# Block-sparse attention with a Strassen-form MLP: batch 1's side steps re-placed, and half of the spread of batches 2 and 3 moved to ScalarE

## The chip, the cores and the metric

One core of a Trainium2 chip runs the kernel. The time is the device time of one execution in microseconds (us), taken as the median of several runs. Engines go by the profile's names: PE is TensorE (matmuls; PEld its weight loads), DVE is VectorE, ACT is ScalarE, POOL is GpSimd, SP is SyncE, which issues DMAs. Each engine works through its own instructions in the order of the program, and waits on semaphores for the others.

## The reference

Four batches, 8 heads, 768 positions, head size 64. Every position attends to the 31 positions around it and to 24 block summaries (maximum of the keys, mean of the values over blocks of 32); then an MLP with a swish gate follows.

```python
k_sum = k.reshape(B, H, nb, block, D).max(axis=3)      # block = 32, nb = 24
v_sum = v.reshape(B, H, nb, block, D).mean(axis=3)
scores_l = scale * q @ k.T, kept where |i - j| < 16
scores_s = scale * q @ k_sum.T + log(block)
a = softmax(concatenate([scores_l, scores_s]))
x = (a @ concatenate([v, v_sum])) -> (B * S, H * D)     # 3072 x 512
h = x @ w_in                                            # 512 x 2048
out = (h * sigmoid(beta * h)) @ w_out                   # 2048 x 512
```

Inputs and output are float32; the kernel multiplies in bf16.

## The kernel before, in words

The batches go one after another. The MLP of batch b fills TensorE, and the attention of batch b+1 is threaded between its output matmuls. Heads go in pairs: four groups g = 0 to 3. Positions go in 12 query tiles of 64, six to a half u = 0, 1.

**The order is written out by hand.** `main` is the list of TensorE's large steps, and `sides` a list of small steps with a place each, from the table `AT`. `run` emits main step i, then every side step whose place is below i + 1 (in the order of the places). A place of 28.05 thus means: behind main step 28. The main steps:

- 0 to 7 `h_two`: two h tiles of batch 0, first half of the positions; step p writes the two-bank tile big1, big2, big0 in turn (p = 7 writes big2, p = 6 big1)
- 8 to 23 `h_half`: 16 h tiles of batch 0, second half, one at a time in one1, big0, one0 in turn
- 24 to 39 `o_atom`: outputs of batch 0, four position tiles (0, 3, 4, 1) in four steps of 4 matmuls each, in one0 or one1; behind the fourth ScalarE copies the result out and SP stores it
- 40 to 46: the last two position tiles of batch 0 as seven products of a Strassen form (`products`, numbered 1, 6, 5, 4, 2, 7, 3)
- from 47 on, 37 steps for each of batches 1, 2 and 3: 16 `h_step` (h tiles of all 768 positions) and 21 products (three tiles t of seven; the first two of t = 0 are `first` and `then`). Batch 1 has 47 to 83, batch 2 84 to 120, batch 3 121 to 157.

Batch 1's attention therefore stands between main steps 8 and 40, batch 2's between 47 and 81, batch 3's between 84 and 117.

PSUM has the single banks one0 and one1, the double banks big1 and big2, and a pair that is big0 during the h tiles and two single banks acc0, acc1 during the products. Product 1 and product 2 share one0, products 6 and 7 one1, product 4 acc0, products 5 and 3 acc1. ScalarE empties products 1, 5 and 2 (`gather`, L683); VectorE the others.

**The side steps that the change touches** (`n` is the batch):

- `kt`, `qt` (`kt_pe` L387, `qt_pe` L396), batch 1 alone: two groups' keys or queries, loaded as whole rows (`krow`, `qrow`, by GpSimd's queue, in `more_loads`), are transposed by TensorE into a double bank, and copied out: keys by VectorE into `kw`, the 96-key windows of each query tile, with 8 copies in all; queries into `qn`, one copy per group by the engine given in `cps`
- `km` (`km_pe` L392): block maxima of one group (VectorE, L357) and their copies into `kw` (GpSimd, L365)
- `vc` (`v_cast`, L456, GpSimd): values to bf16 in `ve`; `vo` (`v_odd_dma`, L466): two DMAs on SP that write the same values 64 positions on into `vo`
- `sc` (`scores`, L429): 12 small matmuls per group and half, u = 0 into big2 and u = 1 into big1; then ScalarE's exponential (L447) into `e`
- `mk` (`mask_e`, L449): VectorE multiplies `e` by the window mask
- `vm` (`vm_all`, L482): block means of the values by TensorE, copied to `vm_sb` by VectorE and ScalarE in turn
- `sp` (`spread`, L492): copies the block means into rows 96 to 127 of `vo` and `ve` for two groups: per call 4 copies of 32 partitions by 768 elements
- `av` (`av_pair`, L865): the value products of one group, 24 matmuls, into big1 for even and big2 for odd groups, then VectorE's normalisation (`norm`, L530) into `xn`
- `xd` (`x_dma`, L550): `xn` transposed into `xT` by a DMA on ScalarE's queue (group 2 of batch 3 by TensorE); `xT` is what the next h tiles read
- `exp`, `silu`: loading of ScalarE's function table; `ws`, `hs`: VectorE's sums for the Strassen form
- `av0`, `x0`: value products and transposes of batch 0's second half; `clear` with `more_masks`: fills and mask

Of the kernel before, what the change touches and what calls it, by code (L numbers as in the profile page):

```python
# [13 lines left out]
    'loads': [2.306],  # L14
    'av0': [1.99, 3.661, 4.754],
    'x0': [5.759, 6.564],
    'scale': [8.171, 16.158, 16.833, 21.634],
    'clear': [6.428, 6.644],
    'kt': [10.122, 8.68],
    'km': [17.109, 13.223, 16.831, 23.85],  # L20
    'qt': [26.508, 26.967],
    'late': [32.254],
    'ws': [23.447, 26.164, 38.352, 39.431],
    'hs0': [36.284, 36.98, 42.604, 40.783],
    'vc1': [26.849, 25.757, 27.058, 30.017],
    'vo1': [27.153, 26.475, 30.624, 30.427],
    'exp1': [26.482],
    'sc1': [28.05, 28.06, 30.05, 30.06, 31.438, 31.448, 33.219, 33.904],
    'mk1': [28.082, 28.092, 30.899, 30.909, 32.558, 32.75, 33.826, 34.448],
    'silu1': [34.957],  # L30
    'vm1': [30.622],
    'sp1': [31.039, 33.384],
    'av1': [35.473, 35.88, 37.299, 37.483],
    'xd1': [36.323, 36.794, 40.874, 39.001],
    'hs1': [52.172, 56.695, 58.36, 62.056, 63.409],
# [13 lines left out]
    'sc2': [64.902, 64.912, 67.132, 67.349, 69.423, 69.507, 71.144, 71.507],  # L49
    'mk2': [64.907, 67.547, 69.019, 69.041, 70.656, 70.74, 74.611, 74.621],  # L50
    'silu2': [83.261],
    'vm2': [69.738],
    'sp2': [70.773, 71.834],
    'av2': [73.1, 73.251, 76.15, 76.759],
# [14 lines left out]
    'exp3': [100.49],  # L69
    'sc3': [100.954, 100.964, 104.012, 104.199, 106.253, 106.263, 107.654, 107.71],  # L70
    'mk3': [101.397, 102.413, 107.921, 107.97, 106.952, 108.221, 108.907, 110.666],
    'silu3': [112.501],
    'vm3': [107.308],
    'sp3': [107.454, 109.743],
    'av3': [110.088, 110.664, 114.187, 114.973],
# [27 lines left out]
def kernel(  # L103
# [10 lines left out]
    nc = tc.nc  # L114
    ctx.enter_context(tc.manual_schedule())
    P = 128
# [14 lines left out]
    J6 = S // P  # L131
# [162 lines left out]
    def more_masks():  # L294
        nc.vector.tensor_copy(out=mask[:], in_=band[:, None, :].to_broadcast([P, NT, QT]))
        nc.vector.memset(mask[0:W, 0], 0.0)
        nc.gpsimd.affine_select(out=mask[:, NT - 1], in_=mask[:, NT - 1], compare_op=ALU.is_ge, fill=0.0,
                                base=QT + W - 1, pattern=[[0, QT]], channel_multiplier=-1)
        nc.vector.memset(mask[NK:NK + nb], 1.0)

# [190 lines left out]

    def spread(gg):  # L492
        r = slice(NK, P)
        s = slice(2 * gg, 2 * gg + 2)
        for tt in (vo, ve):
            for h in range(2):
                nc.vector.tensor_copy(out=tt[r, s, h * J6:(h + 1) * J6, 0:D],
                                      in_=vm_sb[r, h, s, None, :].to_broadcast([P - NK, 2, J6, D]))

# [403 lines left out]
    at("loads", [more_loads])  # L903
    at("av0", [lambda: av_two(0, 1, one), lambda: av_two(2, 1, one[1:]), lambda: av_two(3, 1, one[:1])])
    at("x0", [lambda: x_two(0, 1, dve_cp, one[0]), lambda: x_two(2, 1, dve_cp, one[1])])
# [3 lines left out]
    at("km", [lambda g=g: km_pe(g, nc.gpsimd) for g in range(G)])  # L909
    at("qt", [lambda i=i: qt_pe(1, (2 * i, 2 * i + 1), 1 + i, (dve_cp, act_cp)) for i in range(2)])  # L910
    at("late", [late_tiles])
# [3 lines left out]
    for b in range(1, B):  # L915
# [18 lines left out]
        at("vm" + n, [lambda b=b: vm_all(scope["c"] if b > 1 else big[0], VMC)])  # L934
        at("sp" + n, [lambda i=i: spread(i) for i in range(2)])
        at("av" + n, [lambda g=g, b=b: av_pair(b, g, big[1 + g % 2]) for g in range(G)])
# [34 lines left out]
```

## Time and profile before

| | |
|---|---|
| median of 3 runs | 214.05 us (213.79 to 214.35) |
| profiled execution, its own time | 214.43 us |
| its span, first to last instruction | 211.7 us |
| granted TensorE clock | 0.997 |
| PE busy | 201.2 us (95%) |
| DVE busy | 140.7 us (66%) |
| ACT busy | 118.5 us (56%) |
| POOL busy | 62.3 us (29%) |
| moved by DMA | 33.92 MB, mean 160 GB/s |

Times in the views count from the first instruction. A row of a timeline has start, duration, engine, line of the kernel, operation, what it writes and reads (buffer numbers left out, so that big stands for big0, big1 and big2), partitions and elements, and how many were merged; in brackets the idle time of the engine before it and the instruction that ended it. A DMA that an engine issues is marked with q (ACTq, SPq). In groups by line the two numbers behind the bar are busy us and mean ns of one.

### The profile page before, as it was taken

How to read it: one execution, taken by the hardware profiler on the slowest of the kernel's cores; microseconds unless marked ns; L12 is line 12 of the kernel's file. 1: busy time of each engine (PE TensorE's matmuls, PEld its weight loads, DVE VectorE, ACT ScalarE, POOL GpSimd, SP SyncE). 2: the span in 40 equal slices, each digit the busy share in tenths (PEclk: the TensorE clock that was granted, in tenths of full speed). 3: DMA queues.
4: the chain of work that ended last, by engine and by line, in shares of the span. 5: the costliest groups of instructions: out<-in, count | busy, mean ns of one | idle time of the engine just before them, and what ended most of it. 6: DMA issues, size and time to landing. Idle time of an engine off the chain costs nothing.

```text
span 211.7 us, 5771 instructions
## 1 busy us (share of the span) xinstructions
PE 201.2 (95%) x2387; PEld 140.0 (66%) x2393; DVE 140.7 (66%) x324; ACT 118.5 (56%) x181; POOL 62.3 (29%) x94
## 2 busy tenths in 40 slices
PE   7889999999898999999999999999999999999993
PEld 2477656554545685566888865657788855668882
DVE  4587575899669980858999721998689704464132
ACT  2357876588588113966972138768763129662210
POOL 7708990001720017431520161553401100000111
PEclk9999999999999999999999999999999999999998
DMA  6999999999988988999689969999524920000242
GB/s 119 188 224 177 169 197 191 206 208 213 154 211 206 217 190 214 242 181 214 135 207 235 207 179 292 196 193 188 133 105 29 186 99 3 0 0 3 99 99 99
DMA packets 78393, 33.92 MB, mean 160 GB/s; under 512 B 60688, under 2 KB 75424, under 8 KB 78368
## 3 DMA queue, kind: packets, MB, share of 16 engines
q1 hardware_dynamic: 61968, 23.92, 54.5%
q0 software_dynamic: 7424, 7.34, 21.8%
q10 hardware_dynamic: 8976, 2.30, 7.9%
q8 instruction: 18, 0.29, 0.6%
q14 instruction: 7, 0.06, 0.1%
HBM read 27.37 MB, written 6.29 MB: 159 GB/s over the span
## 4 chain that ended last, share of the span: by engine, by line
PE 70%; DVE 14%; ACT 7%; issue 4%; DMA 3%; POOL 1%; POOLq 0%; DVEq 0%
PE big L601 28%; PE one L665 13%; PE acc L665 9%; PE big L579 5%; ACT e L447 4%; PE one L616 3%; DMA qrow<-in_q_dram 3%; DVE kw L371 2%; PE one L601 2%; DVE qn L371 2%; DVE w_out_sb L337 2%; DVE km L357 2%; DVE e L451 2%; PE big L512 1%; DVE t_sb L646 1%
## 5 line engine op out<-in xcount | busy, mean ns | idle before, releaser
L601 PE MATMUL big<-xT,w_in_sb 128*128 128x384 bf16 x360 | 60.5, 326 | 0.0
L601 PEld LDWEIGHTS <-w_in_sb 128*128 128x128 bf16 x384 | 37.5, 98 | 25.1 <-issue 0.7
L612 ACT ACTIVATE h_sb<-big,beta_sb 128x768 bf16<-128x768 f32 x45 | 39.6, 904 | 25.8 <-PE big L601 25.7
L665 PEld LDWEIGHTS <-h_sb 128*128 128x128 bf16 x320 | 30.7, 98 | 4.9 <-issue 0.5
L646 POOL TENSOR_TENSOR o_sb<-p,u 128x256 f32<-128x256 f32 x10 | 7.3, 728 | 88.7 <-DVE u L646 73.3
L665 PE MATMUL one<-w_out_sb,h_sb 128*128 128x256 bf16 x240 | 30.4, 273 | 0.2 <-ACT p L368 0.2
L447 ACT ACTIVATE e<-big,bias 128x768 bf16<-128x768 f32 x32 | 27.2, 899 | 5.4 <-PE big L426 3.4
L665 PEld LDWEIGHTS <-s_sb 128*128 128x128 bf16 x240 | 23.2, 98 | 2.8
L646 DVE TENSOR_TENSOR s_sb<-h_sb 128x768 bf16<-128x768 bf16 (+2 forms) x16 | 7.8, 488 | 23.4 <-ACT h_sb L612 23.4
L646 DVE TENSOR_TENSOR u<-one,p 128x256 f32<-128x256 f32 x20 | 8.4, 421 | 15.7 <-PE one L665 15.3
L456 POOL CAST ve<-vst 128x832 bf16<-128x832 f32 (+2 forms) x16 | 14.5, 924 | 14.2 <-DMA vst<-in_v_dram 10.8
L368 ACT COPY o_sb<-one 128x256 f32<-128x256 f32 (+1 forms) x14 | 6.1, 433 | 18.4 <-PE one L665 10.1
L451 DVE TENSOR_TENSOR e<-e,mask 128x768 bf16<-128x768 bf16 x24 | 13.4, 584 | 3.8 <-ACT e L447 3.7
L616 PE MATMUL one<-w_out_sb,h_sb 128*128 128x512 bf16 x59 | 14.2, 380 | 0.7 <-issue 0.6
L365 POOL COPY kw<-km 128x288 bf16<-128x288 bf16 x12 | 7.5, 627 | 24.8 <-DVE km L357 14.4
L361 DVE TENSOR_REDUCE km<-kT 128x24 bf16<-128x768 bf16 x12 | 11.3, 945 | 1.9 <-ACT kT L368 1.8
L539 DVE TENSOR_TENSOR xn<-big,r 128x768 bf16<-128x768 f32 x12 | 11.5, 957 | 0.4
L579 PE MATMUL big<-xT,w_in_sb 128*128 128x384 bf16 x64 | 11.6, 327 | 0.0
L665 PE MATMUL acc<-t_sb,h_sb 128*128 128x256 bf16 x80 | 10.9, 273 | 0.0
L646 DVE TENSOR_TENSOR s_sb<-h_sb,s_sb 128x768 bf16<-128x768 bf16 (+2 forms) x16 | 10.1, 630 | 0.5
L665 PE MATMUL one<-t_sb,s_sb 128*128 128x256 bf16 x80 | 10.4, 273 | 0.0
L665 PE MATMUL acc<-t_sb,s_sb 128*128 128x256 bf16 x80 | 10.4, 273 | 0.0
(145 smaller groups left out, 306.1 us busy)
## 6 DMA issues: line engine op xcount, KB each, us to landing
out_dram<-o_sb SPq DMA_DIRECT2D x19, 256.0 KB, 2.6
vst<-in_v_dram SPq DMA_DIRECT2D x13, 336.0 KB, 5.0
kst<-in_k_dram SPq DMA_DIRECT2D x8, 384.0 KB, 5.1
qst<-in_q_dram SPq DMA_DIRECT2D x8, 384.0 KB, 4.5
w_in_sb<-in_moe_w_in_dram POOLq DMA_DIRECT2D x4, 512.0 KB, 7.1
w_out_sb<-in_moe_w_out_dram POOLq DMA_DIRECT2D x4, 512.0 KB, 13.4
vo<-ve SPq DMA_DIRECT2D x12, 107.2 KB, 2.8
vst<-in_v_dram SPq DMA_DIRECT2D x3, 416.0 KB, 8.0
```

Of the source, the lines that this page charges most:

```text
L361: nc.vector.tensor_reduce(out=km[g][:, NK:NK + nb], in_=kT[g][:, W:W + S].rearrange("p (n f) -> p n f", f=block), op=ALU.max, axis=AX.X)
L371: nc.vector.tensor_copy(out=o, in_=i)
L447: nc.scalar.activation(out=e[:], in_=s[:, :, 0:HS], func=ACTF.Exp, bias=bias[:, 0:1], scale=scale)
L451: nc.vector.tensor_mul(out=e.rearrange("p h (m q) -> p h m q", q=QT), in0=e.rearrange("p h (m q) -> p h m q", q=QT), in1=(mask2 if b > 1 e ...
L456: eng.tensor_copy(out=ve[:, g, lo:hi, 0:D], in_=vst[g][:, lo:hi])
L539: nc.vector.tensor_mul(out=x[:, 3 * us[0]:3 * us[0] + 3 * n].rearrange("p (k j) h d -> p k (j h) d", k=n), in0=tv[:, :, :, 0:D], in1=r[:, ...
L579: nc.tensor.matmul(t[:, 0:HS], w_in_sb[:, ki, i * P:(i + 1) * P], xT[:, ki, 0:HS], start=(ki == 0), stop=(ki == k1 - 1))
L601: nc.tensor.matmul(o, w_in_sb[:, ki, i * P:(i + 1) * P], x, start=(ki == 0), stop=(ki == k1 - 1))
L612: nc.scalar.activation(out=o, in_=t, func=ACTF.Silu, scale=beta_sb[:, i:i + 1])
L616: nc.tensor.matmul(t[:, 0:hi - lo], h_sb[:, n, ms * P:(ms + 1) * P], w_out_sb[:, n, lo:hi], start=(n == 0), stop=(n == k2 - 1))
L646: eng.tensor_tensor(out=o, in0=a, in1=b, op=op)
L665: nc.tensor.matmul(SLOTS[n], a[:, j, t * P:(t + 1) * P], b[:, j], start=(j == 0 and n not in (2, 3, 7)), stop=(j == J2 - 1), skip_group_ch ...
```

## The change

The kernel's operations stay, but for one memset that goes from VectorE to GpSimd. What changes is their places, two banks and some engines.

Batch 1: `kt` now turns groups 0, 1 first (behind step 8, in big1) and groups 2, 3 second (behind step 10, in big2), where it was the other way round; `km` follows in the order of the groups. The queries are turned behind step 23, the last h tile, instead of behind step 26; the first two groups in big1, both copied by VectorE, the other two in big0, both copied by ScalarE (before: big1 and big2, with one copy by each engine from each). The casts and shifted copies of the values, the exponential table, the scores, masks, means, spread and value products of batch 1 get new places. The second spread is emitted in two parts (vo, ve). In batch 0 the value products of groups 2 and 3 are joined in one step.

Batches 2 and 3: the second spread (groups 2, 3) goes to ScalarE in two parts, vo behind product 5 of t = 1, ve behind the value products of groups 0, 1. In batch 2 the last two masks move ahead of the value products of groups 0, 1. In batch 3 the first scores go behind the step `then`, and their two masks behind the step after it.

```diff
-    'av0': [1.99, 3.661, 4.754],
+    'av0': [1.99, 4.754],
-    'kt': [10.122, 8.68],
-    'km': [17.109, 13.223, 16.831, 23.85],
-    'qt': [26.508, 26.967],
+    'kt': [8.68, 10.122],
+    'km': [13.223, 16.831, 22.5, 23.85],
+    'qt': [23.5, 23.51],
-    'ws': [23.447, 26.164, 38.352, 39.431],
+    'ws': [25.4, 26.164, 38.352, 39.431],
-    'vc1': [26.849, 25.757, 27.058, 30.017],
-    'vo1': [27.153, 26.475, 30.624, 30.427],
-    'exp1': [26.482],
-    'sc1': [28.05, 28.06, 30.05, 30.06, 31.438, 31.448, 33.219, 33.904],
-    'mk1': [28.082, 28.092, 30.899, 30.909, 32.558, 32.75, 33.826, 34.448],
+    'vc1': [23.52, 24.0, 25.0, 26.0],
+    'vo1': [23.54, 24.1, 25.1, 26.1],
+    'exp1': [23.6],
+    'sc1': [27.05, 27.06, 29.05, 29.06, 31.06, 31.07, 34.05, 34.06],
+    'mk1': [27.6, 27.7, 29.7, 29.8, 31.7, 32.2, 34.7, 34.8],
-    'vm1': [30.622],
-    'sp1': [31.039, 33.384],
-    'av1': [35.473, 35.88, 37.299, 37.483],
-    'xd1': [36.323, 36.794, 40.874, 39.001],
+    'vm1': [31.05],
+    'sp1': [31.2, 32.3, 32.31],
+    'av1': [35.5, 35.6, 38.05, 38.06],
+    'xd1': [36.4, 37.3, 40.3, 39.5],
-    'mk2': [64.907, 67.547, 69.019, 69.041, 70.656, 70.74, 74.611, 74.621],
+    'mk2': [64.907, 67.547, 69.019, 69.041, 70.656, 70.74, 72.6, 72.7],
-    'sp2': [70.773, 71.834],
+    'sp2': [70.773, 72.1, 73.3],
-    'sc3': [100.954, 100.964, 104.012, 104.199, 106.253, 106.263, 107.654, 107.71],
-    'mk3': [101.397, 102.413, 107.921, 107.97, 106.952, 108.221, 108.907, 110.666],
+    'sc3': [101.05, 101.06, 104.012, 104.199, 106.253, 106.263, 107.654, 107.71],
+    'mk3': [102.2, 102.9, 107.921, 107.97, 106.952, 108.221, 108.907, 110.666],
-    'sp3': [107.454, 109.743],
+    'sp3': [107.454, 109.9, 110.9],
...
-        nc.vector.memset(mask[NK:NK + nb], 1.0)
+        nc.gpsimd.memset(mask[NK:NK + nb], 1.0)
...
-    def spread(gg):
+    def spread(gg, cp, ts):
         r = slice(NK, P)
         s = slice(2 * gg, 2 * gg + 2)
-        for tt in (vo, ve):
+        for tt in ts:
             for h in range(2):
-                nc.vector.tensor_copy(out=tt[r, s, h * J6:(h + 1) * J6, 0:D],
-                                      in_=vm_sb[r, h, s, None, :].to_broadcast([P - NK, 2, J6, D]))
+                cp(tt[r, s, h * J6:(h + 1) * J6, 0:D], vm_sb[r, h, s, None, :].to_broadcast([P - NK, 2, J6, D]))
...
-    at("av0", [lambda: av_two(0, 1, one), lambda: av_two(2, 1, one[1:]), lambda: av_two(3, 1, one[:1])])
+    at("av0", [lambda: av_two(0, 1, one), lambda: av_two(2, 1, one)])
...
-    at("qt", [lambda i=i: qt_pe(1, (2 * i, 2 * i + 1), 1 + i, (dve_cp, act_cp)) for i in range(2)])
+    at("qt", [lambda i=i: qt_pe(1, (2 * i, 2 * i + 1), 1 - i, ((dve_cp,) * 2, (act_cp,) * 2)[i]) for i in range(2)])
...
-        at("sp" + n, [lambda i=i: spread(i) for i in range(2)])
+        at("sp" + n, [lambda: spread(0, dve_cp, (vo, ve))] +
+           [lambda t=t, b=b: spread(1, act_cp if b > 1 else dve_cp, (t,)) for t in (vo, ve)])
```

## The prediction

> **What bounds the kernel now.** I read the page first, then the chain of work that ended last, then the timeline of TensorE for idle time, and last the timelines of the engines named as releasers.
>
> ```profile
> span 211.7 us, 5771 instructions
> PE 201.2 (95%) x2387; PEld 140.0 (66%) x2393; DVE 140.7 (66%) x324; ACT 118.5 (56%) x181; POOL 62.3 (29%) x94
> DMA  6999999999988988999689969999524920000242
> ```
>
> TensorE is busy 95% of the span, the next engine 66%. The change takes no matmul away, so it can only give back time in which TensorE waits. The chain shows where it does not wait:
>
> ```profile
> 83.97 15.76 PE big L601 x96
> ```
>
> In the h tiles of a batch (here batch 1's) 96 matmuls follow one another without a hole, so time won before such a stretch stays won. The waits sit between the stretches. In the timeline of TensorE (start, duration, operation, idle time before it and its releaser), batch 1:
>
> ```profile
> 38.76 0.87 PE L384 MATMUL big<-identity,krow 96*64 96x96 bf16 x32 [0.49 <-ACT h_sb L832]
> ...
> 53.09 1.55 PE L384 MATMUL big<-identity,qrow 96*64 96x96 bf16 x64
> 54.57 1.90 PE L616 MATMUL one<-w_out_sb,h_sb 128*128 128x512 bf16 x7
> 57.10 0.53 PE L439 MATMUL big<-qn,kw 64*128 64x64 bf16 x24 [0.63 <-ACT qn L368]
> 57.56 1.90 PE L616 MATMUL one<-w_out_sb,h_sb 128*128 128x512 bf16 x8
> ...
> 59.85 0.58 PE L486 MATMUL big<-ve,A_avg 128*32 128x128 bf16 x28
> ...
> 64.62 0.35 PE L439 MATMUL big<-qn,kw 64*128 64x64 bf16 x12 [0.44 <-ACT e L447]
> ...
> 72.30 1.04 PE L665 MATMUL one<-w_out_sb,h_sb 128*128 128x256 bf16 x8
> ```
>
> Three waits: the key turn for a bank (0.49), the first scores for the queries (0.63), the last scores for a bank that an exponential still reads (0.44). Unit prices from the differences of starts: turning the queries 53.09 to 54.57 = 1.48 us; two output steps (o_atom) from 57.56 to 59.85 less the scores after them = 1.83, so 0.92 each; one pair of scores 57.10 to 57.56 = 0.46; the block means 0.58.
>
> **Batch 1, part by part.** *Key turns swapped.* The turn that now comes first writes big1, whose h tiles were read earlier than those of big2:
>
> ```profile
> 36.02 1.05 ACT L832 ACTIVATE h_sb<-big,beta_sb 128x384 bf16<-128x384 f32 x2 [0.58 <-PE big L579]
> 37.66 1.05 ACT L832 ACTIVATE h_sb<-big,beta_sb 128x384 bf16<-128x384 f32 x2 [0.58 <-PE big L579]
> ```
>
> big1 is free at 37.07, before 38.76 - 0.49 = 38.27, so the 0.49 goes. VectorE copies the same eight pieces in another order, and group 0's maximum comes first. Joining two value products of batch 0 and moving one memset from VectorE to GpSimd change nothing that TensorE waits for: 0.
>
> *Queries turned earlier.* The last h tile ends at 50.41, where the output steps start now, so at 49.92 without the 0.49. The next thing to be late is the load of the queries (issue on GpSimd, then its time to landing):
>
> ```profile
> 50.41 2.75 PE L616 MATMUL one<-w_out_sb,h_sb 128*128 128x512 bf16 x12
> ```
>
> ```profile
> 30.54 0.85 POOL L195 DMA_DIRECT2D qrow<-in_q_dram  x1
> ```
>
> ```profile
> qrow<-in_q_dram POOLq DMA_DIRECT2D x1, 768.0 KB, 19.6
> ```
>
> It lands at 30.54 + 19.6 = 50.14: TensorE waits 0.2. Behind the turn, each of VectorE and ScalarE copies two groups:
>
> ```profile
> 51.03 1.28 ACT L744 ACT_TABLE_LOAD   x1
> 55.39 1.66 ACT L368 COPY qn<-big 128x768 bf16<-128x768 bf16 x2 [2.86 <-DVE qn L371]
> 57.49 1.69 ACT L447 ACTIVATE e<-big,bias 128x768 bf16<-128x768 f32 x2
> ```
>
> The turn ends at 50.14 + 1.48 = 51.62; ScalarE's copies end near 53.3, and the table load, now behind them, near 54.8. Four output steps cover TensorE until 51.62 + 4 x 0.92 = 55.3. So the 0.63 goes; without that cover the first exponential would wait for the table. From 55.3 on: scores 0.46, two steps 1.83, scores, two steps, means 0.58, scores, three steps 2.75; the last scores start at 63.6. Each pair needs the banks of the pair before, which the two exponentials leave 0.39 + 1.69 = 2.08 after that pair's start (57.49 - 57.10, and the row's 1.69); the pairs stand 0.46 + 1.83 = 2.29 apart or more.
>
> *A new wait.* One output step (0.92) now stands between the last scores and the first value products, which write big1. The bank is free at 63.6 + 2.08 = 65.7, TensorE there at 63.6 + 0.46 + 0.92 = 65.0. It waits 0.7. Then two value products, three steps, two value products, one step:
>
> ```profile
> 66.81 0.88 PE big L512 x48
> ```
>
> 65.7 + 0.9 + 2.75 + 0.9 + 0.92 = 71.2, where the products of L665 stood at 72.30: **1.1 us** won. The second pair of value products waits for VectorE's normalisation today; three steps instead of two hide that. Covers: the means need the last cast of v,
>
> ```profile
> 58.42 1.30 POOL L456 CAST ve<-vst 128x832 bf16<-128x832 f32 x1 [1.17 <-ACT e L447]
> ```
>
> which ends at 59.72 and is needed at 59.86: 0.1 spare, at the price of its lateness. On GpSimd the first cast now stands ahead of group 3's key sums, on SP all eight copies to vo ahead of batch 0's first output and batch 2's first key load; nobody needs these within 5 us. Ends for batch 1: 0 (queries land 1.1 later) to 1.8 (no wait of 0.7).
>
> **Batches 2 and 3.** Four copies (vo, ve of groups 2, 3) go from VectorE to ScalarE. Batch 2, TensorE, then ScalarE, then VectorE:
>
> ```profile
> 115.70 0.22 PE L512 MATMUL big<-ve,e 128*64 128x65 bf16 x1
> ...
> 117.25 1.05 PE L665 MATMUL one<-w_out_sb,h_sb 128*128 128x256 bf16 x8
> ```
>
> ```profile
> 111.82 0.38 ACT L368 COPY p<-acc 128x256 f32<-128x256 f32 x1
> 114.84 1.24 ACTq L554 DMA_TRANSPOSE xT<-xn  x1
> 116.18 0.37 ACT L368 COPY o_sb<-one 128x256 f32<-128x256 f32 x1 [3.98 <-DMA kst<-in_k_dram]
> 116.25 1.23 ACTq L554 DMA_TRANSPOSE xT<-xn  x1
> ```
>
> ```profile
> 115.86 1.02 DVE L451 TENSOR_TENSOR e<-e,mask 128x768 bf16<-128x768 bf16 x2
> ```
>
> The value products should take 0.9 from 115.70 to 116.6 and end at 117.25, because both masks come at 115.86: 0.65 lost. The change puts these masks ahead of the normalisation and takes the four copies out of VectorE. The nearest prices:
>
> ```profile
> L497 DVE COPY vo<-vm_sb 32x768 bf16<-32x768 bf16 x12 | 3.8, 353 | 0.1
> ```
>
> ```profile
> L368 ACT COPY qn<-big 128x768 bf16<-128x768 bf16 x3 | 2.4, 798 | 2.9 <-DVE qn L371 2.9
> L368 ACT COPY vo<-ve 32x384 bf16<-32x384 bf16 x1 | 0.5, 509 | 0.0
> ```
>
> No row shows ScalarE copying 768 elements from SBUF: between 0.80 (same count, from PSUM) and 2 x 0.51 = 1.02. I take 0.85, near the row of the same count. The copies run from 112.20 (111.82 + 0.38) to 112.20 + 3.4 = 115.6, just ahead of 115.70. Behind them on ScalarE stand the transposing DMA (1.24) and the copy (0.37) that frees bank one0 for the product at 117.25. That DMA's issue can begin beside the last copy, as at 116.25 (0.07 after a copy began): 114.8 + 1.24 + 0.37 gives 116.4, early enough. So batch 2 wins **0.65**; at 1.02 the value products start at 116.3 and it wins 0.05.
>
> The Trainium skill ("ScalarE: Activation LUTs", What ACT_TABLE_LOAD costs) gives 186 ns + 0.833 ns per element for an instruction with immediate operands, less 93 ns back to back: an estimate of 0.73 per copy, at which batch 3 below would win 0.35 more and the sum would be 211.5. Its 826 ns for one agrees with the 798 above to 4%.
>
> Batch 3, TensorE, then ScalarE:
>
> ```profile
> 145.20 0.64 PE L436 MATMUL big<-qn,kw 64*128 64x64 bf16 x24
> ...
> 148.85 1.03 PE L665 MATMUL one<-w_out_sb,h_sb 128*128 128x256 bf16 x8 [0.17 <-ACT p L368]
> ...
> 160.78 1.04 PE L665 MATMUL one<-w_out_sb,h_sb 128*128 128x256 bf16 x8
> 161.75 0.22 PE L512 MATMUL big<-ve,e 128*64 128x65 bf16 x1
> ...
> 163.16 1.03 PE L665 MATMUL one<-t_sb,s_sb 128*128 128x256 bf16 x8
> ```
>
> ```profile
> 148.43 0.37 ACT L368 COPY p<-one 128x256 f32<-128x256 f32 x1
> 156.99 0.37 ACT L368 COPY p<-acc 128x256 f32<-128x256 f32 x1
> ```
>
> The first scores move behind a product. They took 0.64 where others take 0.52, so they waited 0.12 for a bank; and the copy of p at 148.43 no longer stands behind their exponentials, so the 0.17 goes: 0.3 won. Further on, the four copies run from 157.36 to 160.76, then 0.37 for the copy that frees one0: 161.13, where the product stands at 160.78. A new wait of 0.35; then value products 0.97 later, and 0.9 more to 163.0 against 163.16: **0.15** won, since VectorE, 4 x 0.35 = 1.4 lighter, no longer holds them. Together 0.45; at 1.02 per copy -0.2, at 0.80 +0.65.
>
> **Sum:** 1.1 + 0.65 + 0.45 = 2.2 us. The profiled execution took 214.43, so 212.2; the median of the runs is 214.05, 0.38 less, so **211.85**. Some 0.3%, 0.64 us, is what a measurement here tells from no change.
>
> **The rivals.** *A: ScalarE becomes the bound (slower).* At a price c per copy batch 2 wins 117.25 - (112.2 + 4c + 0.9) once c is over 0.87, batch 3 wins 0.45 - 4(c - 0.85). With 1.1 from batch 1 the change is even at c = 1.14 and past 0.3% slower from 1.22; at 1.3 it gives 214.05 + 1.3 = 215.35. Against it: 798 ns for the same count, 1.02 as twice the half. For it: VectorE does the same copy in 353 ns. The skill's same page (Rules for kernel authors) would leave plain arithmetic on VectorE, up to about 3 times faster in bf16; the rows here give 2.4 for c = 0.85. Chance 0.08.
>
> *B: the queries land later.* The DMA line is at 9 and 8 for most of the span, and the turn has lost the 53.09 - 50.14 = 2.95 us of slack that it had. Landing 1.1 later takes batch 1's gain: 212.95. With c = 0.90 besides, batch 2 wins 0.55 and batch 3 0.25: 213.25. Chance 0.22.
>
> *C: given back.* Batch 2's loads share that full DMA line; if they do not move along with TensorE, its scores wait for them and what batches 1 and 2 won is spent there, so that 0.45 is left: 213.6, no change that a measurement can tell. Against it: most of them are issued behind casts and stores that TensorE's own progress releases. Chance 0.08.
>
> **How the numbers follow.** The forecast has 0.62. Faster takes the forecast and B, 0.84; C is the same, 0.08; A slower, 0.08. The range leaves out A and C: up to 213.4 (0.65 won), and down to 210.8 (batch 1 with 1.8, batch 3 with 0.65, batch 2 as it is, 3.1 won, and 0.15 for the measurement).
>
> **What would show it.** Right: no idle time before the first key turn; the queries' turn right behind the last h tile with an idle time of about 0.2 put down to the DMA of qrow; none before the first scores; a new idle time near 0.7 before the first value products of batch 1, put down to an exponential; L497 gone for half its copies and four copies of vo and ve per batch on ScalarE near 0.85; in batch 3 a wait near 0.35 for a copy of o_sb. Wrong: copies over 1.1 us, the turn waiting over 1 us, or new idle time before the first scores of batches 2 and 3.

## The result and the profile after

Beside each other on one chip the kernel before took 214.35 us (median of 11 runs, 213.69 to 215.01) and the changed kernel 212.61 us (11 runs, 211.63 to 215.52): a ratio of 0.9921, with a 95% interval of 0.9893 to 0.995. (Ratios leave out disturbed executions; medians and ranges hold all.) The forecast was 211.85 with a range of 210.8 to 213.4. The profiled execution of the changed kernel took 211.63 us, the lowest of the eleven, with a span of 209.9.

The page of the changed kernel, its first rows (line numbers from about 497 on are one lower than before):

```profile
span 209.9 us, 5777 instructions
PE 200.3 (95%) x2387; PEld 140.0 (67%) x2393; DVE 139.4 (66%) x315; ACT 124.6 (59%) x189; POOL 63.3 (30%) x95
PEclk9969999999999999999999999999999999999999
```

ScalarE has 6.1 us more to do (118.5 before) and VectorE 1.3 less. The sum of what each engine does tells nothing of the 1.8 us by which the span is shorter; the stages do. These are the starts and ends of TensorE's stretches, subtracted (us; the h tiles of batches 1 and 2 are counted to the start of their last matmul):

| stage of TensorE | before | after | forecast of the difference |
|---|---|---|---|
| start to the h tiles of batch 0's second half | 37.45 | 38.05 | 0 |
| those h tiles with batch 1's key turns | 12.94 | 12.38 | -0.49 |
| to the first scores of batch 1 | 6.71 | 5.85 | -1.33 |
| to the products of batch 0's last position tiles | 15.20 | 15.71 | +0.7 |
| to the h tiles of batch 1 | 6.30 | 6.23 | 0 |
| h tiles of batch 1 | 20.81 | 20.85 | 0 |
| between the h tiles of batches 1 and 2 | 23.96 | 23.42 | -0.65 |
| h tiles of batch 2 | 20.81 | 20.82 | 0 |
| between the h tiles of batches 2 and 3 | 24.56 | 23.64 | -0.45 |
| h tiles of batch 3 and the rest | 42.97 | 42.97 | 0 |

The head, up to the h tiles of batch 0's second half, is 0.60 longer in this execution. TensorE waits 1.71 us there for the first keys (0.41 in the profile of before), and from 12 to 15 us its granted clock is half:

```profile
10.44 0.53 PE L384 MATMUL one<-identity,krow 96*64 96x96 bf16 x16 [1.71 <-DMA krow<-in_k_dram]
```

```profile
12.00:15.00 3.00, 3.00 (x47) 2.46 (x45) 2.38 (x4) 0.42 (x3) 0.00 (x0) 0.50 1.17 245
```

(A row of the windows has start and end, length, the busy time of PE, PEld, DVE, ACT and POOL, the granted clock, the busy share of the DMA engines and GB/s.) That is the first sign that loads from memory move from run to run by more than the effects in question. One part of the head is shorter: from its first h tile on it takes 12.59 us (25.46 to 38.05) instead of 12.81 (24.64 to 37.45).

Batch 1, timeline of TensorE in the changed kernel:

```profile
38.79 0.87 PE L384 MATMUL big<-identity,krow 96*64 96x96 bf16 x32
...
51.24 1.55 PE L384 MATMUL big<-identity,qrow 96*64 96x96 bf16 x64 [0.81 <-DMA qrow<-in_q_dram]
52.72 3.63 PE L615 MATMUL one<-w_out_sb,h_sb 128*128 128x512 bf16 x15
56.28 0.52 PE L439 MATMUL big<-qn,kw 64*128 64x64 bf16 x24
...
66.65 0.19 PE L511 MATMUL big<-ve,e 128*64 128x65 bf16 x1 [0.64 <-ACT e L447]
```

The 0.49 before the key turn is gone. The queries' turn stands right behind the last h tile and waits 0.81, not 0.2. Nothing is idle before the first scores. The new wait before the first value products is there, 0.64 where 0.7 was forecast, and it is put down to an exponential.

Batch 2, ScalarE and then VectorE in the changed kernel:

```profile
112.01 1.56 ACT L368 COPY vo<-vm_sb 32x768 bf16<-32x768 bf16 x2
113.47 1.55 ACT L368 COPY ve<-vm_sb 32x768 bf16<-32x768 bf16 x2
114.24 1.23 ACTq L553 DMA_TRANSPOSE xT<-xn  x1
115.56 0.37 ACT L368 COPY o_sb<-one 128x256 f32<-128x256 f32 x1 [0.54 <-PE acc L664]
```

```profile
112.06 1.02 DVE L451 TENSOR_TENSOR e<-e,mask 128x768 bf16<-128x768 bf16 x2
```

Four copies go from 112.01 to 115.02, 0.6 earlier than the forecast's 115.6. The transposing DMA's issue does begin beside the last copy, as argued. VectorE's last masks come 3.80 us earlier than the 115.86 of before. The value products now run from 115.49 to 116.37, 0.88 instead of 1.55.

At the start of the batch VectorE's copy of `kw` takes longer. VectorE before and after, then GpSimd before and after:

```profile
103.83 0.45 DVE L371 COPY kw<-kT 128x1152 bf16<-128x1152 bf16 x1
```

```profile
102.94 1.13 DVE L371 COPY kw<-kT 128x1152 bf16<-128x1152 bf16 x1
```

```profile
100.72 2.98 POOL L456 CAST ve<-vst 128x832 bf16<-128x832 f32 x3 [1.22 <-DMA vst<-in_v_dram]
```

```profile
100.97 2.78 POOL L456 CAST ve<-vst 128x832 bf16<-128x832 f32 x3 [1.81 <-DMA vst<-in_v_dram]
```

Before, GpSimd's last cast ended at 103.70, ahead of the copy; after, it runs beside it until 103.75. In the fourteen profiles the copy takes 1.13 in the seven with a cast beside it (the change, 1, 5, 6, 7, 8, 12) and 0.45 in the seven without.

Batch 3, TensorE and ScalarE in the changed kernel:

```profile
145.31 0.52 PE L436 MATMUL big<-qn,kw 64*128 64x64 bf16 x24
...
147.52 1.04 PE L664 MATMUL one<-w_out_sb,h_sb 128*128 128x256 bf16 x8
...
159.52 1.03 PE L664 MATMUL one<-w_out_sb,h_sb 128*128 128x256 bf16 x8
...
161.37 1.05 PE L664 MATMUL one<-t_sb,s_sb 128*128 128x256 bf16 x8
```

```profile
156.05 1.56 ACT L368 COPY vo<-vm_sb 32x768 bf16<-32x768 bf16 x2
157.52 1.55 ACT L368 COPY ve<-vm_sb 32x768 bf16<-32x768 bf16 x2
...
159.10 0.37 ACT L368 COPY o_sb<-one 128x256 f32<-128x256 f32 x1
```

The first scores take 0.52 and no longer 0.64; the product at 147.52 has no idle time; the copy that frees one0 ends at 159.47, and the product that needs it starts at 159.52. Its predecessor could have let it go at 159.46 (158.58 and 0.88), so the forecast wait of 0.35 is 0.06.

### The profile page after: what moved, and what is told of

The parts are those of the page before. It is cut to its first block, busy times and chain, and to the rows that moved or that the text cites. A ratio compares the mean times of both kernels' runs of the same rounds, so it can differ in the third digit from the quotient of the medians.

```text
span 209.9 us, 5777 instructions
## 1 busy us (share of the span) xinstructions
PE 200.3 (95%) x2387; PEld 140.0 (67%) x2393; DVE 139.4 (66%) x315; ACT 124.6 (59%) x189; POOL 63.3 (30%) x95
## 4 chain that ended last, share of the span: by engine, by line
PE 70%; DMA 16%; POOL 5%; DVE 2%; issue 2%; ACT 1%; SPq 1%; POOLq 0%
PE big L600 28%; PE one L664 16%; PE acc L664 12%; DMA qrow<-in_q_dram 10%; PE one L615 6%; DMA krow<-in_k_dram 3%; DMA vst<-in_v_dram 3%; PE big L511 3%; PE one L600 2%; POOL w_out_sb L334 1%; PE big L436 1%; POOL w_in_sb L331 1%; SPq L216 1%; POOL vo L463 1%; ACT e L447 1%
## 5 line engine op out<-in xcount | busy, mean ns | idle before, releaser
L645 DVE TENSOR_TENSOR s_sb<-h_sb 128x768 bf16<-128x768 bf16 (+2 forms) x16 | 8.5, 529 | 23.2 <-ACT h_sb L611 23.2
L456 POOL CAST ve<-vst 128x832 bf16<-128x832 f32 (+2 forms) x16 | 15.1, 963 | 13.9 <-DMA vst<-in_v_dram 13.9
L451 DVE TENSOR_TENSOR e<-e,mask 128x768 bf16<-128x768 bf16 x24 | 14.4, 625 | 2.0 <-ACT e L447 1.8
```

Of the source, the lines that this page charges most:

```text
L451: nc.vector.tensor_mul(out=e.rearrange("p h (m q) -> p h m q", q=QT), in0=e.rearrange("p h (m q) -> p h m q", q=QT), in1=(mask2 if b > 1 e ...
L456: eng.tensor_copy(out=ve[:, g, lo:hi, 0:D], in_=vst[g][:, lo:hi])
L645: eng.tensor_tensor(out=o, in0=a, in1=b, op=op)
```

## The experiments

A diff shows the changed kernel's line and then the experiment's, unless another base is named. The ratios are to the kernel before on the same chip. Their results in the profiles come first, since most verdicts are read across kernels. "Landing" is the landing of the queries' load against the end of batch 0's last h tile; the next columns are the stages of the table above.

| kernel | landing | to first scores | to products | to h tiles of batch 1 | batches 1-2 | batches 2-3 | median |
|---|---|---|---|---|---|---|---|
| before | -0.22 | 6.71 | 15.20 | 6.30 | 23.96 | 24.56 | 214.35 |
| the change | +0.76 | 5.85 | 15.71 | 6.23 | 23.42 | 23.64 | 212.61 |
| 1 batch 1 alone | +0.82 | 5.90 | 15.71 | 6.96 | 24.10 | 24.56 | 214.83 |
| 2 batches 2, 3 alone | +0.53 | 7.37 | 15.20 | 6.30 | 23.35 | 23.65 | 214.06 |
| 3 spread on VectorE | +2.51 | 7.60 | 15.71 | 6.23 | 24.63 | 24.75 | 214.52 |
| 4 turn one step later | +1.41 | 5.63 | 16.08 | 6.23 | 23.31 | 23.65 | 211.45 |
| 5 last scores earlier | +2.09 | 7.18 | 14.99 | 7.37 | 23.54 | 23.66 | 212.26 |
| 6 copies twice | +1.12 | 6.21 | 15.70 | 6.24 | 25.92 | 28.03 | 218.39 (one run) |
| 7 queries loaded first | -1.23 | 4.97 | 16.66 | 6.47 | 23.42 | 23.66 | 213.59 |
| 8 the change again | +1.88 | 6.96 | 15.71 | 6.24 | 23.43 | 23.66 | 212.82 |
| 9 values released earlier | -1.60 | 4.98 | 16.92 | 7.14 | 23.30 | 23.66 | 212.70 |
| 10 turn one step later again | -0.53 | 5.15 | 15.71 | 6.23 | 23.29 | 23.66 | 212.14 |
| 11 turn later, loads moved | -2.19 | 5.15 | 15.71 | 6.71 | 23.30 | 23.65 | 213.02 |
| 12 swap and batches 2, 3 | +1.62 | 7.69 | 15.23 | 6.30 | 23.43 | 23.65 | 212.86 |

The last two stages repeat closely: wherever ScalarE makes the four copies once it is 23.3 to 23.5 and 23.65, elsewhere 23.96 and 24.56 or more. Those of batch 1 move by 2 us and more, and the medians with them, so that intervals are 0.3 to 0.5% to either side.

Two stages are not in the table. The head takes from 36.58 us (5) to 39.90 (10) in the fourteen profiles, a wider scatter than that of any stage of batch 1. In six of them (the change, 1, 8, 9, 10, 11) TensorE runs there at half its granted clock for about 3 us. And in 4 and 7 the h tiles of batch 1 are 0.42 and 1.54 longer than in the other profiles, with waits of 0.26 and 1.38 for the transposed x, and in 7 those of batch 2 0.41.

**1. Batch 1 alone.** The spread of batches 2 and 3 back on VectorE, with their old places.

```
-           [lambda t=t, b=b: spread(1, act_cp if b > 1 else dve_cp, (t,)) for t in (vo, ve)])
+           [lambda t=t, b=b: spread(1, dve_cp, (t,)) for t in (vo, ve)])
```

> Batch 1's part of the change alone; batches 2 and 3 as before. Theory W (each batch gives back its own waits): the waits of 0.49, 0.63 and 0.44 us go, one of 0.64 before the first value products and one for the landing of the queries (0.81 in the changed kernel's trace) come. Net 0.3 to 1.1 us faster, so ratio 0.995 to 0.9985, and batches 2 and 3 show the old waits for VectorE's masks. Theory S (all of the gain is VectorE's relief in batches 2 and 3): ratio 1.000, since the wait for the queries takes what the others gave.

Measured: 214.83 us, 1.0018 (0.9988 to 1.0047). The profile has the key turn without wait, the 0.64, and a wait of 0.86 for the queries. One more was not foreseen:

```profile
52.34 1.55 PE L384 MATMUL big<-identity,qrow 96*64 96x96 bf16 x64 [0.86 <-DMA qrow<-in_q_dram]
77.43 1.80 PE L664 MATMUL one<-w_out_sb,h_sb 128*128 128x256 bf16 x15 [0.68 <-ACT p L368]
```

The copy of p stands on ScalarE behind the issue of a transposing DMA, which took 2.32 us there and 1.30 in the profile of the change. Batch 1 alone brings nothing that this comparison can tell, as theory S had it and not W.

**2. Batches 2 and 3 alone.** All places, banks and engines of batches 0 and 1 as before.

```
-    'kt': [8.68, 10.122],
+    'kt': [10.122, 8.68],
...
-    'qt': [23.5, 23.51],
+    'qt': [26.508, 26.967],
...
-    'sc1': [27.05, 27.06, 29.05, 29.06, 31.06, 31.07, 34.05, 34.06],
+    'sc1': [28.05, 28.06, 30.05, 30.06, 31.438, 31.448, 33.219, 33.904],
```

> The part for batches 2 and 3 alone; batch 1 as before. Theory W: batch 2 wins about 0.65 us at the second pair of value products, batch 3 about 0.9 us (0.45 at the first scores, 0.45 at the value products), together 1.5 us, ratio 0.993, with the waits of batch 1 where they were before. Theory S: all of the change's gain, ratio 0.992. The two theories are told apart by this run's sum with the other part: under W the two parts add up to more than this one alone.

Measured: 214.06 us, 0.9973 (0.9938 to 1.0009). Batches 2 and 3 are those of the change to 0.1 us (0.61 and 0.91 less than before). Ahead of them, the wait before batch 1's first scores was 1.29 instead of 0.63: the first quarter of w_out landed 0.95 later than in the profile of before (39.26 to 38.31), and VectorE, which scales it and then copies keys and queries, ran late by as much. The profile has the 1.5 us of theory W; the median of the runs has half of it, which is taken up in the account below.

**3. The spread of batches 2 and 3 on VectorE, all else changed.** The same diff as in 1, but with the new places of the masks and scores.

> The whole change with its new places, but the second spread of batches 2 and 3 back on VectorE at the same places. Theory W: at the new places VectorE copies ve behind two normalisations, so the second value products wait about 1.1 us in batch 2 (ve copied near 116.6 instead of 115.0) and 0.9 us in batch 3; ratio to the kernel before about 1.001, to the change 1.009. Theory P (the new places of the masks do the work, the engine does not matter): the same time as the change, 0.992.

Measured: 214.52 us, 1.0004 (0.997 to 1.0037). TensorE:

```profile
116.89 0.19 PE L511 MATMUL big<-ve,e 128*64 128x65 bf16 x1 [1.02 <-DVE ve L371]
162.99 0.19 PE L511 MATMUL big<-ve,e 128*64 128x65 bf16 x1 [0.86 <-DVE ve L371]
```

Without the other engine the new places of the masks put the copies themselves in the path, at 1.02 and 0.86 us where theory W had 1.1 and 0.9; P falls. The places alone lose; the places and the engine together win.

**4. The queries' turn behind the first output step.**

```
-    'qt': [23.5, 23.51],
+    'qt': [24.5, 24.51],
```

> The change with the queries turned one output step later (behind step 24 instead of 23). Theory W, with the landing of the queries as the cause of the wait before their turn: the step of 0.9 us fills the wait of 0.8, the scores come at the same place behind step 27, so 0.5 to 0.8 us faster than the change, ratio to the kernel before about 0.989, with no idle time before the turn. Theory L (the wait is a cost of the turn itself, or comes back before the scores): the idle time moves to the turn or to the first scores and the time is that of the change, 0.992.

Measured: 211.45 us (6 runs), 0.9854 (0.9814 to 0.9894). The queries landed 1.41 after the last h tile, and the turn waited 0.41 only, since a step of 0.92 stood ahead of it. Up to the products 0.37 was lost again (16.08 instead of 15.71), 0.15 of it in a wait for the last cast of v.

**5. The last scores of batch 1 one step earlier,** its copies of the block means all on VectorE.

```
-    'sc1': [27.05, 27.06, 29.05, 29.06, 31.06, 31.07, 34.05, 34.06],
+    'sc1': [27.05, 27.06, 29.05, 29.06, 31.06, 31.07, 33.05, 33.06],
...
-        at("vm" + n, [lambda b=b: vm_all(scope["c"] if b > 1 else big[0], VMC)])
+        at("vm" + n, [lambda b=b: vm_all(scope["c"] if b > 1 else big[0], VMC if b > 1 else [dve_cp] * 4)])
```

> The change with batch 1's last pair of scores one output step earlier (two steps instead of one between them and the first value products) and, so that ScalarE is free for their exponentials, all four copies of the sums of v on VectorE. Theory W (each hole that the trace names costs its own length): the idle time of 0.64 before the first value products goes to 0, products of batch 1's last tile start 0.6 earlier after the first scores (15.71 in the change, 15.1 here), 0.6 us or 0.3% less in all. Rival G (the hole is only moved): the pair one step earlier meets a bank that the pair before still holds; the idle time then stands before the last scores, 0.5 to 0.6 long, and the time is that of the change within 0.2 us.

Measured: 212.26 us (4 runs), 0.9899 (0.9856 to 0.9941). The 0.64 went, and the products came 0.72 earlier after the first scores. Then TensorE met the next two:

```profile
74.34 1.03 PE L664 MATMUL acc<-t_sb,h_sb 128*128 128x256 bf16 x8 [0.44 <-DVE t_sb L645]
75.88 1.91 PE L664 MATMUL one<-w_out_sb,h_sb 128*128 128x256 bf16 x16 [0.50 <-ACT p L368]
```

VectorE's last masks begin at 66.16 (66.20 in the change) and the sum t_sb at 73.08 (73.13): VectorE goes without a pause from 61.5 on and had nothing earlier to give. Neither theory held whole: the hole costs its length where it stands, and VectorE takes it back eight microseconds on.

**6. The copies of groups 2 and 3 twice.** Nothing is left out; the second copies write the same values again.

```
-           [lambda t=t, b=b: spread(1, act_cp if b > 1 else dve_cp, (t,)) for t in (vo, ve)])
+           [lambda t=t, b=b: spread(1, act_cp if b > 1 else dve_cp, (t, t) if b > 1 else (t,)) for t in (vo, ve)])
```

> The change with the four copies to vo and ve of groups 2 and 3 done twice in batches 2 and 3, all on ScalarE: eight instead of four, the second four writing the same values again. Theory A (the copies stand in the path at their own pitch, 0.735 us each): in batch 2 ScalarE ends them at 117.9 instead of 115.0, the last value products start there instead of 115.5, 2.4 us later; in batch 3 the copy that frees bank one0 ends 2.9 later, at 162.4, and the product that stands at 159.52 waits for it, 2.8 more; span about 5.2 us longer, both idle times put down to ScalarE. Rival H (ScalarE had room, the copies are hidden): the time lengthens by under 2 us.

Measured: one run, 218.39 us; span 216.7, 6.8 longer than that of the change. TensorE:

```profile
117.16 0.19 PE L511 MATMUL big<-ve,e 128*64 128x65 bf16 x1 [1.73 <-ACT ve L368]
117.89 0.19 PE L511 MATMUL big<-ve,e 128*64 128x65 bf16 x1 [0.51 <-ACT ve L368]
...
164.83 1.87 PE L664 MATMUL one<-w_out_sb,h_sb 128*128 128x256 bf16 x8 [2.83 <-ACT o_sb L368]
```

Both places are those that the forecast's chain named, and batch 2 is 2.50 longer (2.4 expected). Batch 3 is 4.39 longer, 1.5 more than the wait. The windows of that stretch show the granted clock:

```profile
core 0: us, PE busy (x) PEld busy (x) DVE busy (x) ACT busy (x) POOL busy (x), PEclk, DMA share, GB/s
162.00:164.80 2.80, 0.00 (x0) 0.00 (x0) 1.61 (x5) 2.76 (x6) 0.73 (x1) 1.00 0.15 29
164.80:166.60 1.80, 1.77 (x8) 0.98 (x7) 0.00 (x0) 1.49 (x2) 0.00 (x0) 0.50 1.07 256
166.60:168.05 1.45, 1.45 (x49) 1.39 (x48) 0.47 (x2) 0.37 (x1) 0.00 (x0) 0.50 0.59 139
168.05:169.01 0.96, 0.96 (x13) 0.81 (x9) 0.93 (x3) 0.00 (x0) 0.00 (x0) 0.92 1.19 196
```

In this execution TensorE rests 2.83 us and then runs at half its clock: the product takes 1.80 instead of 0.97, the value products 1.46 instead of 0.88, together 1.4 of the 1.5.

**7. The queries loaded ahead of the last quarter of w_out.**

```
-    'scale': [8.171, 16.158, 16.833, 21.634],
+    'scale': [8.171, 16.158, 16.833, 23.7],
...
-        wo.append(load_w_out(3))
         wo.append(sw_load(qrow, q, 1, 0, 8))
+        wo.append(load_w_out(3))
```

> The change with the load of batch 1's queries issued ahead of the last quarter of w_out instead of behind it, and that quarter's scaling on VectorE moved behind the copies of the queries. Theory L (the place in the load queue sets when the turn starts): the queries land 2.5 to 4 us earlier, at 47 to 49; no idle time before their turn; the first scores start 5.1 to 5.2 after the end of the last h tile instead of 5.85; 0.8 us or 0.4% less than the change, in a run whose head is quick up to 2 us less. Rival R (the bytes in front of the turn stay the same, and the last quarter is now the late one): it lands at 50 to 52, its scaling ends near 54 and the fourth output step, which reads it, waits as long as the turn did: 0.5 to 0.8 idle there, and no gain.

Measured: 213.59 us (10 runs, 210.98 to 214.56), 0.989 (0.984 to 0.9941). The landing came 1.23 ahead of the last h tile's end, the turn waited for nothing and the scores started 4.97 behind it. Then:

```profile
59.96 0.56 PE L486 MATMUL big<-ve,A_avg 128*32 128x128 bf16 x25 [0.74 <-POOL ve L456]
...
81.69 0.81 PE L600 MATMUL big<-xT,w_in_sb 128*128 128x384 bf16 x4 [1.38 <-DMA xT<-xn]
```

What the turn won is spent on the last cast of v and, inside the h tiles of this execution, on the transposed x. Of the two theories L told the turn, R the fate of the gain, but at another place than R named.

**8. The change again,** unaltered.

> The change itself once more, beside the three others on one chip. Theory L (the landing of the queries, which moves from run to run, sets the start of batch 1's scores): the idle time before the queries' turn differs from the 0.81 of the first profile by what the landing lies earlier or later against the end of the last h tile, and the first scores start 5.1 us behind the landing again; if the queries have landed by that end, no idle time and 5.0 from the end. Rival F (the 0.81 is a fixed cost of the new order): 0.8 again wherever the load lands.

Measured: 212.82 us (10 runs), 0.9906 (0.987 to 0.9941).

```profile
52.54 1.55 PE L384 MATMUL big<-identity,qrow 96*64 96x96 bf16 x64 [1.92 <-DMA qrow<-in_q_dram]
54.02 3.63 PE L615 MATMUL one<-w_out_sb,h_sb 128*128 128x512 bf16 x16
57.58 0.52 PE L439 MATMUL big<-qn,kw 64*128 64x64 bf16 x24
```

The same kernel waits 1.92 here and 0.81 before; the load landed at 52.50, 5.08 ahead of the first scores, against 51.19 and 5.09. The landing sets the start; the wait is no fixed price. In 1, 3, 5 and 6, where the load is late too, the scores start 5.09 behind it as well, so that what is won ahead of the turn only lengthens its wait. In this execution batch 1 has won nothing over before: 12.38 + 6.96 + 15.71 + 6.24 = 41.29, against 41.15 (and its head, not in these sums, is 0.79 longer).

**9. The values released earlier,** on top of 7.

```
-                behind(i, wo[3])
+                behind(i, wo[2])
```

> The queries' load ahead of the last quarter of w_out, as in the run before, and the loads of v released behind the third quarter (44.4 there) instead of behind the queries (48.2). Theory V (what took the gain back was the last cast of v, 0.74 idle before the means, because v is loaded behind the queries): the cast ends 2 us earlier, no idle time before the means, none before the queries' turn, the first scores 5.0 and the products of batch 0's last tile 20.9 us after the end of the last h tile (21.56 in the change, 21.63 in the run before); 0.6 us less than the change, 0.3%. Rival X (the loads share one line, so that v earlier means queries later): the queries land 1 to 2 us later than 48.2 and the turn waits 0.3 to 1 us; no gain. Rival D (the next limit takes it): the waits in this stage go, and the transposed x of batch 1 comes late for the h tiles as it did there (1.38 idle); no gain.

Measured: 212.70 us (6 runs), 0.9891 (0.9854 to 0.9928). Theory V falls. SyncE, the issues of the loads of v, and TensorE:

```profile
44.20 0.33 SPq L210 DMA_DIRECT2D vst<-in_v_dram  x1
44.57 2.69 SPq L211 DMA_DIRECT2D vst<-in_v_dram  x1
47.37 0.39 SPq L210 DMA_DIRECT2D vst<-in_v_dram  x1
47.80 3.92 SPq L211 DMA_DIRECT2D vst<-in_v_dram  x1
51.82 0.39 SPq L210 DMA_DIRECT2D vst<-in_v_dram  x1
```

```profile
60.51 0.56 PE L486 MATMUL big<-ve,A_avg 128*32 128x128 bf16 x25 [0.93 <-POOL ve L456]
```

The first load is issued 4.1 us earlier than in 7 (48.28), but the issues that follow are held for 2.69 and 3.92, and the last values land at 59.10 instead of 58.88. The queries were not later (48.12 to 48.21), so X falls too. In these two executions the order of release made no difference to the end of the loads; that the DMA line sets that end is likely, and not shown.

**10. The turn behind one step, beside the change on one chip** (the kernel of 4).

> The queries' turn behind the first output step, as in the fourth run (211.45), now beside the change on one chip. Theory L: one step of 0.9 covers a landing up to 0.9 us after the last h tile, so the idle time of the turn is 0.8 to 0.9 less for the same landing; against the change on this chip 0.5 to 0.9 us less, 0.3 to 0.4%. Rival N (the fourth run was only a run with quick loads): within 0.3 us of the change.

Measured: 212.14 us (6 runs), 0.9875 (0.9836 to 0.9913), 0.68 below the change on the same chip. Behind the head there is no wait in this profile but the 0.64. Its intervals overlap those of the change both times, so the step is likely and not proven; it has the lowest median of the kernels measured beside it both times.

**11. Turn and loads together:** the lines of 7 and 9, the turn of 4, the last quarter scaled at 23.4.

> Both: the queries loaded ahead of the last quarter of w_out, v released behind the third, and the turn behind the first output step, with that quarter's scaling ahead of the copies of the queries. Theory L with V: no idle time before the turn in any run, none before the means; 20.9 us from the end of the last h tile to the products; 0.6 to 0.9 us less than the change and not over 0.2 from the turn behind one step alone, since one step already covers most landings. Rival K (the scaling of the last quarter, 1.2 us on VectorE and waiting for its landing near 51, now stands ahead of the copies of the queries): the first scores wait for them, 0.3 to 1 us, and it is no faster than the change.

Measured: 213.02 us (6 runs), 0.9901 (0.9863 to 0.9939). Two waits are gone and the first scores do not wait for the scaling, so K's wait did not come; 0.40 before the value products, now put down to VectorE, and 0.48 more behind the products take their place. It measured no faster than 10, but all six of its executions had a granted clock below 0.996 (three of six in 10), so the two medians don't compare like with like.

**12. The key turns swapped, and batches 2 and 3, without the early queries:** the kernel of 2 with two lines of the change.

```
-    'kt': [10.122, 8.68],
-    'km': [17.109, 13.223, 16.831, 23.85],
+    'kt': [8.68, 10.122],
+    'km': [13.223, 16.831, 22.5, 23.85],
```

> The kernel before with the swapped key turns of batch 1 and with batches 2 and 3 of the change, but the queries of batch 1 turned and copied where they were before. Theory T (earlier turning of the queries is worth nothing on the mean of runs, because what it wins is spent on the landing of the load and before the value products: 21.6 and 22.7 us from the end of the last h tile to the products in the two profiles of the change, 21.9 before): no idle time before the key turn, 12.4 us for the h tiles around it, batches 2 and 3 as in the change (23.4 and 23.65 between their h tiles), the rest of batch 1 as before; 0.55 + 0.55 + 0.9 = 2.0 us less than before, ratio 0.991, the same as the change. Rival Q (the turn carries part of the gain, and the two parts measured alone are to be added to the swap): the ratio of the second run, 0.997, less 0.25% for the swap, 0.9945, so 0.7 to 0.9 us slower than the change. Rival Y (the h tiles that end 0.5 earlier meet VectorE, which scales w_out and copies keys until the queries' copies can start): the swap's 0.55 comes back as idle time before the first scores, over 1.0 instead of 0.63, and the ratio is 0.994.

Measured: 212.86 us (10 runs), 0.9911 (0.9877 to 0.9944). The time is T's, the trace is Y's. TensorE, ScalarE:

```profile
57.46 0.53 PE L439 MATMUL big<-qn,kw 64*128 64x64 bf16 x24 [1.61 <-POOL ve L456]
```

```profile
55.74 1.66 ACT L368 COPY qn<-big 128x768 bf16<-128x768 bf16 x2 [3.84 <-DVE qn L371]
```

The h tiles took 12.38 again, and the idle time before the first scores grew from 0.63 to 1.61. (It is put down to a cast that ended at 57.45; the scores need ScalarE's copies, which ended at 57.40.) In the old order, then, VectorE sets the first scores, and the landing of w_out sets VectorE. So the 0.56 of the swap is not won here. Experiments 2 and 12 have spans of 210.8 and 210.7, and their ratios differ by 0.6%: so much a comparison of medians here can be off.

## Why the prediction was right, and where it was not

The time fell into the range and on the right side, 0.76 above the forecast. That the sum came so near is partly luck: of batch 1's 1.1 little was kept, and two terms that were put too low, batch 3 and the value products of batch 0, made up for some of it. By its own steps:

- *Joined value products of batch 0:* put at 0 ("change nothing that TensorE waits for"), and worth 0.22. From the first h tile to the end of the head TensorE takes 12.59 us in all eleven profiles that have the joined step, and 12.81 in all three that don't (before, 2, 12). No wait of TensorE is shown in that stretch in the profile of before or of the change, so the moved memset has no part in it.
- *Key turns swapped:* right for the wait, 0.56 for 0.49 in every kernel that has the swap but 3 (0.44). It was counted as won, and that is not shown: in 12 it came back before the first scores, and in the change a late load takes it.
- *Queries turned earlier:* the mechanism was right, and the term was mis-sized. "It lands at 30.54 + 19.6 = 50.14: TensorE waits 0.2" took one landing of the profile of before as fixed. The change took the slack of 2.95 away, and with it the cover for a load that, at its old place in the queue, lands anywhere from 0.53 before (10) to 2.51 after the last h tile (3; the change itself 0.76 and 1.88). The wait was 0.81 and 1.92. More of that scatter is the head's than the load's: the eleven loads at the old place land between 50.17 and 52.50 us, while the end of the last h tile moves from 48.95 to 52.28. A quick head waits for the load. This is rival B, "the queries land later", which had a chance of 0.22 and a price of 1.1 us: it is the rule rather than the exception. The prediction's own sign of being wrong, "the turn waiting over 1 us", came in 3, 5, 6 and 8.
- *A new wait* of 0.7 before the value products: right, 0.64 in nine profiles to the hundredth. The last value products: right, hidden.
- *The means and the last cast of v,* "0.1 spare, at the price of its lateness": right, and part of the reason why an earlier turn doesn't pay (0.74 in 7, 0.93 in 9).
- *Batch 1 in sum:* -0.98 in the first profile for the forecast's -1.1, +0.14 in the second. The gain is what the load leaves over. The first figure flatters the change, since a longer head had covered part of the load there. From the first instruction to the products of batch 0's last position tiles the five profiles with batch 1's part of the change as it is (the change, 1, 3, 6, 8) take 71.90 to 73.29 us, 72.55 in the mean, and the three with the old places (before, 2, 12) 72.30 to 72.91, 72.63 in the mean.
- *Batch 2:* 0.54 for 0.65. The value products gave 0.67; 0.13 went to a wait of product 1 for VectorE at 104.92, not foreseen. It comes with VectorE's long copy of `kw`: where ScalarE makes the four copies once, the stage is 23.42 to 23.54 with a copy of 1.13 us and 23.29 to 23.35 with one of 0.45.
- *Batch 3:* 0.92 for 0.45, the other mis-sized term. The copies' price was taken at 0.85 and is 0.735 from start to start, so the wait of 0.35 is 0.06 (0.29 more won), and the first scores brought 0.45 up to there instead of 0.3. By the Trainium skill ("ScalarE: Activation LUTs", What ACT_TABLE_LOAD costs), whose figures are for an ACTIVATE, an estimate for the copy is 0.826 alone and 0.73 in a row; the profile has 0.82 and 0.735. That estimate was the better one. The row at hand, 798 ns with reads from PSUM, was the length of one copy; its only pair starts 0.87 apart.
- *The rivals:* A falls at this price, but its chain and its two places were exact when the work was doubled (6). C didn't come: the stages between h tiles keep their 23.3 to 23.5 and 23.65 in every kernel with the copies on ScalarE once, however late they begin.

The sum by stages is then 1.46 from batches 2 and 3, shown by all kernels that have their part, and from batches 0 and 1 something between 1.0 and nothing. The measured 1.74 (and 1.9 in the second comparison) lies within that.

That batch 1 alone measured 1.0018 and batches 2 and 3 alone 0.9973, which do not add to 0.9921, has an explanation in the granted clock. Every profile with a stretch at half clock has a mean granted clock of 0.989 to 0.992, every other 0.996 or more. The same figure is on record for each execution, and it divides them. Median in us, with the number of executions, of those that the ratios use:

| kernel, chip | clock 0.996 or more | lower |
|---|---|---|
| before, first chip | 214.26 (22) | 215.47 (6) |
| 1 batch 1 alone | 214.30 (6) | 215.29 (6) |
| 2 batches 2, 3 alone | 212.52 (4) | 214.39 (8) |
| before, second chip | 214.59 (9) | 215.43 (5) |
| 8 the change again | 212.50 (4) | 213.30 (5) |
| before, third chip | 214.07 (8) | 215.18 (6) |
| 12 swap and batches 2, 3 | 212.62 (5) | 213.13 (4) |

Eight of the twelve executions of 2 were of the lower kind, against six of 28 of before beside them. Within one kind batches 2 and 3 bring 1.1 to 1.7 us (1.5 to 2.1 in 12), batch 1 alone between nothing and 0.2, and the change 2.1. With as few as four executions in a group this is a reading and not a proof, but it puts the gain where the stages show it: in batches 2 and 3. Whether a kernel's order makes the half clock in the head more frequent is open.

## What to carry to other kernels

A step that is moved up against a load loses its slack, and a single profile shows one landing, not the latest one: leave a step of other work ahead of it, as in experiment 10, where 0.9 us of cover cost nothing behind it. Work moved to an idle engine is priced by the start-to-start time of a row of them and by who stands behind the last one on that engine. When a hole is closed, look for the next late thing a few microseconds on: what 5, 7 and 12 closed was given back there. Before medians are compared, see whether the executions had the same granted clock.

## What the runs showed of the hardware that was not expected

- TensorE rested 2.83 us in 6 and was then granted 0.50 of its clock for 3.25 us; rests of 1.73 to 2.56 in 6, 5 and 3 did not bring it down (1.00 in the window behind the 2.56). So a wait of 2.8 cost 4.4. The length of the rest alone does not decide: in the heads of six profiles rests of 1.51 to 2.19 (1.71 in the change) were followed by 0.50 for about 3 us. What else decides is not shown. The Trainium skill ("TensorE: Matmul & The Clock Gate", Part 1: The HAM clock gate) gives the half rate for a TensorE that was idle for a window of about 3.4 us; the half agrees, the rest here was shorter.
- The issue of one transposing DMA held ScalarE between 1.23 and 2.32 us, and the copies behind it with it (waits of TensorE for such a copy: 0.68 in 1, 0.50 in 5).
- A load of 768 KB behind 2 MB on GpSimd's queue landed at 50.17 in the profile of before, and at 51.19 and 52.50 in the two profiles of the change.
- The same VectorE copy (128x1152, bf16) took 0.45 us alone and 1.13 beside a cast on GpSimd, seven profiles each without an exception.
